# Attention with q and k laid out transposed on the host, and products of 48 instead of 64 columns

## The chip, the cores and the metric

The program runs on one core of a Trainium2 chip. The metric is the device time of one execution in microseconds (us). The engines are named as in the profile: PE (TensorE, with its weight loads as PEld), DVE (VectorE), ACT (ScalarE), POOL (GpSimd) and SP (SyncE, which here issues most of the DMAs). Every engine works through its own instructions in the order in which the program was written.

## The reference

Three parts follow each other. The first is a delta-rule attention over 4 batches, 8 heads, 768 steps and 48 dimensions; the second and third are a routed mixture of experts (8 experts, 2 per token) and a dense layer of 2048 hidden units.

```python
k_n = k / (np.linalg.norm(k, axis=-1, keepdims=True) + 1e-06)
for t in range(S):
    kt, vt, bt = (k_n[:, :, t], v[:, :, t], beta[:, :, t, None])
    y[:, :, t] = np.einsum('bhd,bhde->bhe', q[:, :, t], state)
    v_old = np.einsum('bhde,bhd->bhe', state, kt)
    state = state + bt[:, :, :, None] * np.einsum('bhd,bhe->bhde', kt, vt - v_old)
...
x = np.ascontiguousarray(attn_out.transpose(0, 2, 1, 3)).reshape(B * S, H * D)
x = _moe_ref(x=x, **moe_kwargs)
return _moe2_ref(x=x, **moe2_kwargs)
```

## The kernel before

The attention is computed in blocks of 64 steps. There are 12 such blocks in a sequence, and two batches share a block's work (one in partitions 0 to 63, one in 64 to 127), so 24 blocks n = 0 to 23 are done, and even and odd n are two independent recurrences. Per block the program does the following, each step a function in emit_attention.

- load_kq (L166) brings q and k of the block in as tiles kq, with the step in the partition. trans (L191) turns four heads at a time on PE (L197) and copies them out of PSUM into mq (two copies, L201, on ACT). So mq holds q and k with the head dimension in the partition. A block takes two calls of trans.
- gram (L203), two calls per block, multiplies k by q and k (L214). ACT copies the q part into mq (two copies, L219) and the k part into gd and goff (L222, L223). DVE then adds the second half into gd (L224); this last step is put off until the next flush. The PSUM tiles gm have two buffers.
- inverse_ops (L242) inverts the 32 x 32 triangular blocks of four n on DVE (head L256, the products L296 and L304, the tail L321 and L322). Its some 130 instructions are spread between the other work by run(t), which hands out credit according to the table PE_US, times PACE; what is left is put out at the end of each group of four blocks. merge1 and merge2 combine two 32-blocks (PE L347 and L368, DVE L370).
- The recurrence is ks (L389), solve (L399) and update (L410), and output (L422) gives y; each is 16 matrix products, 32 PE instructions, and ACT copies their results out of PSUM. In ks, solve and output 64 columns move, of which 48 are used; in update 48 move.
- v_norm (L377) and the mask (L237) run on POOL; the router's transposes, logits and the DVE steps of the routing (L820 on) are mixed in. warm (L434) puts unneeded matrix products on PE; the tables F, FG and FL say how many and where.

At the start the first four blocks are loaded, turned and multiplied, POOL fills the constant halves of mq (init_m, L120) and clears T (L255), and the inverse of the first four blocks runs while grams of blocks 4 to 7 are done (20.6 to 59 us). Then the loop over n in steps of two does the recurrence for n and n + 1 and the gram of n + 8 and n + 9. From 310 us on come the last four blocks and the handover to the experts, and from 385 us on the experts and the dense layer, in which PE is nearly always busy.

Of the kernel before, what the change touches and what calls it, by code (L numbers as in the profile page):

```python
# [16 lines left out]
DP = 64  # L17
# [9 lines left out]
TA = 2  # L27
# [11 lines left out]
PE_US = dict(ks=1.26, solve=1.26, update=1.0, output=1.26, trans=0.43, gram=0.94, merge1=0.6, merge2=0.6)  # L39
# [52 lines left out]
def emit_attention(ctx, tc, q, k, v, beta, const, rt, moe):  # L92
# [11 lines left out]
    NK, NQ, NM, NU = 4, 4, 10, 4  # L104
    tok = [slice(0, 64), slice(64, 128)]
    st = [slice(64, 128), slice(0, 64)]
    kbd = [pk.tile([128, NH, 2, HD], F32, name=f"kbd{i}") for i in range(NK)]
    kq = [pr.tile([128, NH, 2, DP], F32, name=f"kq{i}") for i in range(NQ)]
    mq = [[(pr if i >= 4 else pk).tile([128, NH, 2, CH], F32, name=f"mq{b}{i}") for i in range(NM)] for b in range(2)]
    us = [[pk.tile([128, NH * HD + 16], F32, name=f"us{b}{i}") for i in range(NU)] for b in range(2)]  # L110
    rz = [[pk.tile([128, NH * HD + 16], F32, name=f"rz{b}{i}") for i in range(2)] for b in range(2)]

    def init_k(i):
        for b in range(2):
            nc.vector.tensor_copy(out=kbd[i][st[b], :, b, :],
                                  in_=eye[st[b], 0:HD].unsqueeze(1).to_broadcast([64, NH, HD]))

    def init_m(i):
        for b in range(2):
            nc.gpsimd.affine_select(out=mq[b][i][tok[b], :, 1, :],  # L120
# [4 lines left out]
    for i in range(NQ):  # L125
        (nc.vector if i < 2 else nc.gpsimd).memset(kq[i][:, :, :, HD:DP], 0.0)
# [10 lines left out]
    def cols(t, h):  # L137
        return t[:, h * HD:h * HD + 64]
# [379 lines left out]
    for n in range(4):  # L518
        load_kq(n)
# [1105 lines left out]
```

## Time and profile before

| | us |
|---|---|
| median of 3 runs | 1234.82 |
| lowest and highest run | 1229.9 and 1238.5 |
| span of the profiled execution | 1245.6 |
| busy in it: PE, DVE, ACT, POOL | 1163.7, 711.4, 548.2, 311.6 |

The page gives no other time for the profiled execution than its span; it lies outside the three timed runs, 10.8 us above their median. Busy times are averages over parts with different limits, so they have to be read by stretch. In a wait row the left side is the engine and line that stood still, the right side what it was waiting for last.

### The profile page before, as it was taken

How to read it: one execution, taken by the hardware profiler on the slowest of the kernel's cores; microseconds unless marked ns; L12 is line 12 of the kernel's file. 1: busy time of each engine (PE TensorE's matmuls, PEld its weight loads, DVE VectorE, ACT ScalarE, POOL GpSimd, SP SyncE). 2: the span in 40 equal slices, each digit the busy share in tenths (PEclk: the TensorE clock that was granted, in tenths of full speed). 3: DMA queues.
4: the chain of work that ended last, by engine and by line, in shares of the span. 5: the costliest groups of instructions: out<-in, count | busy, mean ns of one | idle time of the engine just before them, and what ended most of it. 6: DMA issues, size and time to landing. Idle time of an engine off the chain costs nothing. (4 is left out here: it accounts for less than half of the span.)

```text
span 1245.6 us, 26717 instructions
## 1 busy us (share of the span) xinstructions
PE 1163.7 (93%) x10743; PEld 1051.9 (84%) x10760; DVE 711.4 (57%) x1923; ACT 548.2 (44%) x1133; POOL 311.6 (25%) x399
## 2 busy tenths in 40 slices
PE   7798888787878999999999999989999999999998
PEld 4476767665757999999999999978989898998988
DVE  7988789879363777675757453436242433425150
ACT  5776777763453433232324233337242433434150
POOL 7242244555244513232231313015000000000000
PEclk9998899988889999999999999999999999999999
DMA  4634334322325545444534321262202010110000
GB/s 85 103 79 92 66 73 92 73 40 42 91 77 190 159 161 173 164 144 155 188 136 160 116 90 56 67 200 78 70 7 64 13 60 17 45 33 2 24 1 26
DMA packets 146530, 109.47 MB, mean 88 GB/s; under 512 B 110104, under 2 KB 131941, under 8 KB 145638
## 3 DMA queue, kind: packets, MB, share of 16 engines
q1 hardware_dynamic: 137446, 86.39, 25.1%
q0 software_dynamic: 8448, 19.70, 4.9%
q8 instruction: 85, 1.39, 0.5%
q10 hardware_dynamic: 512, 1.67, 0.4%
q14 instruction: 39, 0.32, 0.1%
HBM read 82.43 MB, written 26.08 MB: 87 GB/s over the span
## 5 line engine op out<-in xcount | busy, mean ns | idle before, releaser
L1197 PE MATMUL yp<-w2h,ht 128*128 128x384 f32 x832 | 221.2, 340 | 0.0
L1197 PE MATMUL yp<-w2l,ht 128*128 128x384 f32 x448 | 150.2, 335 | 0.0
L1197 PEld LDWEIGHTS yp<-w2h,ht 128*128 128x128 f32 x832 | 148.5, 188 | 0.3
L987 POOL DMA_INDIRECT y<-ys,idp x56 | 65.0, 1161 | 301.8 <-DVE ys L1206 223.5
L1174 PE MATMUL hp<-xth,w1h 128*128 128x416 f32 (+2 forms) x384 | 136.9, 357 | 0.6 <-ACT xth L1115 0.6
L1174 PE MATMUL hp<-xtl,w1h 128*128 128x416 f32 (+2 forms) x384 | 136.2, 355 | 0.0
L1174 PE MATMUL hp<-xth,w1l 128*128 128x416 f32 (+2 forms) x384 | 135.8, 354 | 0.0
L1535 PE MATMUL yp<-woh,gh 128*128 128x384 f32 x384 | 130.4, 340 | 0.0
L1535 PE MATMUL yp<-woh,gl 128*128 128x384 f32 x384 | 129.1, 336 | 0.0
L1535 PE MATMUL yp<-wol,gh 128*128 128x384 f32 x384 | 129.1, 336 | 0.0
L1177 ACT ACTIVATE ht<-hp 128x416 fp32r<-128x416 f32 (+2 forms) x128 | 66.4, 519 | 133.1 <-PE hp L1174 118.4
L1180 DVE SCALAR_TENSOR_TENSOR ht<-hp,ht 128x352 fp32r<-128x352 f32 (+3 forms) x192 | 79.3, 441 | 63.5 <-ACT ht L1177 61.3
L1503 PE MATMUL hp<-xh,wih 128*128 128x512 f32 x288 | 112.8, 392 | 2.7 <-DVE three L1489 2.7
L304 DVE TENSOR_TENSOR T<-T,tmp 128x1 f32<-128x1 f32 (+9 forms) x540 | 113.8, 258 | 0.4
L1503 PE MATMUL hp<-xl,wih 128*128 128x512 f32 x288 | 112.9, 392 | 0.0
L1503 PE MATMUL hp<-xh,wil 128*128 128x512 f32 x288 | 112.7, 391 | 0.0
L1512 DVE TENSOR_TENSOR gl<-r,gh 128x512 fp32r<-128x512 f32 x96 | 66.5, 693 | 78.4 <-ACT gh L1511 78.4
L1506 ACT ACTIVATE r<-hp,three 128x512 f32<-128x512 f32 x96 | 66.2, 690 | 89.0 <-PE hp L1503 89.0
L1508 DVE SCALAR_TENSOR_TENSOR r<-r,hp 128x512 f32<-128x512 f32 x96 | 65.4, 681 | 53.9 <-ACT r L1506 53.9
L1197 PEld LDWEIGHTS yp<-w2l,ht 128*128 128x128 f32 x448 | 84.1, 188 | 0.0
L214 PE MATMUL gm<-mq 64*64 64x128 f32 (+1 forms) x896 | 60.8, 266 | 19.6 <-ACT mq L201 11.0
L1542 ACT ACTIVATE os<-yp 128x384 f32<-128x384 f32 x23 | 11.3, 492 | 153.4 <-PE yp L1535 153.4
(221 smaller groups left out, 2300.5 us busy)
## 6 DMA issues: line engine op xcount, KB each, us to landing
r<-in_moe_w_dram SPq DMA_DIRECT2D x16, 768.0 KB
r<-in_moe_w_dram SPq DMA_DIRECT2D x21, 512.0 KB
yg<-y SPq DMA_DIRECT2D x24, 384.0 KB
wd_r<-in_moe_w_in_dram SPq DMA_DIRECT2D x6, 1024.0 KB
wd_r<-in_moe_w_out_dram SPq DMA_DIRECT2D x8, 768.0 KB
kq<-in_q_dram SPq DMA_DIRECT2D x48, 96.0 KB
kq<-in_k_dram SPq DMA_DIRECT2D x48, 96.0 KB
v<-in_v_dram SPq DMA_DIRECT2D x48, 96.0 KB
```

Of the source, the lines that this page charges most:

```text
L214: nc.tensor.matmul(gm[tok[b], h, lo:hi], lhsT=m[:, 1, :], rhs=m[:, lo // 64:hi // 64, :], start=True, stop=True)
L304: nc.vector.tensor_tensor(out=T[:, lo:hi, 0:w], in0=T[:, lo:hi, 0:w], in1=tmp[jj % 2][:, (lo - w) * w:(hi - w) * w].rearrange("p (t k) -> ...
L987: return nc.gpsimd.indirect_dma_start(out=y, out_offset=bass.IndirectOffsetOnAxis(ap=idx, axis=0), in_=src, in_offset=None, bounds_check=y ...
L1174: nc.tensor.matmul(p[:, 0:w], lhsT=a[:, k, fs], rhs=b[:, k, c], start=(i == 0), stop=(i == 3 * KD - 1))
L1177: nc.scalar.activation(out=h[:, c], in_=p[:, 0:w], func=ACTF.Relu)
L1180: nc.vector.scalar_tensor_tensor(out=h[:, rest(lo, hi)], in0=p[:, lo - c.start:hi - c.start], scalar=0.0, in1=h[:, lo:hi].bitcast(F32), op ...
L1197: nc.tensor.matmul(p[0:2 * m if pair else m, 0:DM], lhsT=a, rhs=b[:, f, :], start=f == i == 0, stop=f == FT - 1 and i == len(terms) - 1)
L1503: nc.tensor.matmul(p, lhsT=a[:, k, fs], rhs=b[:, k, :], start=(i == 0), stop=(i == 3 * KD - 1))
L1506: nc.scalar.activation(out=r, in_=p, func=ACTF.Relu, bias=three)
L1508: nc.vector.scalar_tensor_tensor(out=r, in0=r, scalar=6.0, in1=p, op0=ALU.min, op1=ALU.mult)
L1512: nc.vector.tensor_tensor(out=gl[:, f, :], in0=r, in1=gh[:, f, :].bitcast(F32), op=ALU.subtract)
L1535: nc.tensor.matmul(p[:, 0:DM], lhsT=a[:, f, c], rhs=b[:, f, :], start=(i == 0), stop=(i == 3 * FT2 - 1))
```

## The change

The host now lays the inputs out. q and k arrive as one array with the head dimension in the rows (48 rows, padded with zeros to 64 for the first 12 blocks), and load_qk writes them straight into mq. The function trans and its copies go, and so do the tiles kq and what cleared them. mq is kept for 12 blocks instead of 10, and init_m runs for each of them; q and k now lie in two separate halves of the tile. ks, solve and output move 48 columns instead of 64. k, v, beta, the noise and the router's weights come in the order in which the tiles hold them, with fewer loads. The entry for trans leaves the table PE_US; PACE, F, FG, FL and the counts of warm are as they were.

```diff
-TA = 2
...
-PE_US = dict(ks=1.26, solve=1.26, update=1.0, output=1.26, trans=0.43, gram=0.94, merge1=0.6, merge2=0.6)
+PE_US = dict(ks=1.26, solve=1.26, update=1.0, output=1.26, gram=0.94, merge1=0.6, merge2=0.6)
...
-    NK, NQ, NM, NU = 4, 4, 10, 4
+    NK, NM, NU = 4, 12, 4
     tok = [slice(0, 64), slice(64, 128)]
     st = [slice(64, 128), slice(0, 64)]
-    kbd = [pk.tile([128, NH, 2, HD], F32, name=f"kbd{i}") for i in range(NK)]
-    kq = [pr.tile([128, NH, 2, DP], F32, name=f"kq{i}") for i in range(NQ)]
-    mq = [[(pr if i >= 4 else pk).tile([128, NH, 2, CH], F32, name=f"mq{b}{i}") for i in range(NM)] for b in range(2)]
-    us = [[pk.tile([128, NH * HD + 16], F32, name=f"us{b}{i}") for i in range(NU)] for b in range(2)]
-    rz = [[pk.tile([128, NH * HD + 16], F32, name=f"rz{b}{i}") for i in range(2)] for b in range(2)]
+    kbd = [pk.tile([128, 2, NH, HD], F32, name=f"kbd{i}") for i in range(NK)]
+    mq = [[(pk if i in [n % NM for n in range(NT - 4, NT)] else pr).tile([128, 2, NH, CH], F32, name=f"mq{b}{i}") for i in range(NM)] for b in range(2)]
+    us = [[pk.tile([128, NH * HD], F32, name=f"us{b}{i}") for i in range(NU)] for b in range(2)]
+    rz = [[pk.tile([128, NH * HD], F32, name=f"rz{b}{i}") for i in range(2)] for b in range(2)]
...
-    for i in range(NQ):
-        (nc.vector if i < 2 else nc.gpsimd).memset(kq[i][:, :, :, HD:DP], 0.0)
...
-        return t[:, h * HD:h * HD + 64]
+        return t[:, h * HD:(h + 1) * HD]
...
-    def bp_c(n):
-        return n % 2, n // 2
-
     def load_k(n):
-        bp, c = bp_c(n)
         for b in range(2):
-            nc.sync.dma_start(out=kbd[n % NK][tok[b], :, b, :],
-                              in_=k[2 * bp + b, :, c * CH:(c + 1) * CH, :].rearrange("h t d -> t h d"))
-
-    def load_kq(n):
-        bp, c = bp_c(n)
-        for i, src in enumerate((q, k)):
-            for b in range(2):
-                nc.sync.dma_start(out=kq[n % NQ][64 * i:64 * i + 64, :, 1 - b, 0:HD],
-                                  in_=src[2 * bp + b, :, c * CH:(c + 1) * CH, :].rearrange("h t d -> t h d"))
+            nc.sync.dma_start(out=kbd[n % NK][tok[b], b], in_=k[n, b])
+
+    def load_qk(n, part=slice(0, 2)):
+        rows = 64 if n < NM else HD
+        for b in range(2):
+            nc.sync.dma_start(out=mq[b][n % NM][st[b].start:st[b].start + rows, part], in_=qk[n, b, 0:rows, part])
 
     def load_v(n):
-        bp, c = bp_c(n)
         t = wk.tile([128, NH, HD], F32, tag="v", name="v", bufs=4)
-        for b in range(2):
-            nc.sync.dma_start(
-                out=t[tok[b]], in_=v[2 * bp + b, :, c * CH:(c + 1) * CH, :].rearrange("h t d -> t h d"))
+        nc.sync.dma_start(out=t, in_=v[n])
         vt[n] = t
 
     def load_beta(g):
         t = wk.tile([128, 32], F32, tag="beta", name="beta")
-        for cc in range(2):
-            for b in range(2):
-                for blk in range(2):
-                    s0 = (2 * g + cc) * CH + blk * 32
-                    p0 = b * 64 + blk * 32 + cc * 16
-                    nc.sync.dma_start(
-                        out=t[p0:p0 + 16, :],
-                        in_=beta[:, :, s0:s0 + 32].rearrange("(bp b) h t -> b bp h t", b=2)[b])
+        nc.sync.dma_start(out=t, in_=beta[g])
         beta_t[g] = t
-
-    def trans(n, hh):
-        first = n < 4
-        tp = ps2.tile([128, 4, 2, CH], F32, tag="ch" if first and hh else "tp", name="tp")
-        for h in range(4):
-            nc.tensor.transpose(tp[:, h].rearrange("p k t -> p (k t)"),
-                                kq[n % NQ][:, 4 * hh + h].rearrange("p k d -> p (k d)"), ident)
-        for b in range(2):
-            copy = nc.vector.tensor_copy if first and hh else nc.scalar.copy
-            copy(out=mq[b][n % NM][st[b], 4 * hh:4 * hh + 4], in_=tp[st[b]])
 
...
-                m = mq[b][n % NM][st[b], 4 * hh + h]
+                m = mq[b][n % NM][st[b], :, 4 * hh + h]
...
-                nc.scalar.copy(out=mq[b][n % NM][tok[b], hs, 0, :], in_=gm[tok[b], :, 0:64])
+                nc.scalar.copy(out=mq[b][n % NM][tok[b], 0, hs, :], in_=gm[tok[b], :, 0:64])
...
-                nc.tensor.matmul(p[tok[b], h, :], lhsT=mq[b][n % NM][:, h, 1, :], rhs=cols(us[b][n % NU], h),
+                nc.tensor.matmul(p[tok[b], h, 0:HD], lhsT=mq[b][n % NM][:, 1, h, :], rhs=cols(us[b][n % NU], h),
...
-                nc.tensor.matmul(p[tok[b], h, :], lhsT=x[:, h, :], rhs=cols(rz[b][n % 2], h), start=True, stop=True)
+                nc.tensor.matmul(p[tok[b], h, 0:HD], lhsT=x[:, h, :], rhs=cols(rz[b][n % 2], h), start=True, stop=True)
...
-                nc.tensor.matmul(p[o:o + HD, h, 0:HD], lhsT=kbd[n % NK][:, h, b, :], rhs=cols(us[b][n % NU], h)[:, 0:HD],
+                nc.tensor.matmul(p[o:o + HD, h, 0:HD], lhsT=kbd[n % NK][:, b, h, :], rhs=cols(us[b][n % NU], h),
...
-                nc.tensor.matmul(p[tok[b], h, :], lhsT=mq[b][n % NM][:, h, 0, :], rhs=cols(us[b][n % NU], h),
+                nc.tensor.matmul(p[tok[b], h, 0:HD], lhsT=mq[b][n % NM][:, 0, h, :], rhs=cols(us[b][n % NU], h),
...
     for n in range(4):
-        load_kq(n)
+        load_qk(n, slice(1, 2))
     load_beta(0)
-    for i in range(2, NM + 2):
-        init_m(i % NM)
+    for n in range(4):
+        load_qk(n, slice(0, 1))
+    for i in range(NM):
+        init_m(i)
     warm(P0)
-    for i in range(TA):
-        trans(*divmod(i, 2))
     for i in range(8):
-        if TA > 1:
-            flush()
-        if i + TA < 8:
-            trans(*divmod(i + TA, 2))
         flush()
         gram(*divmod(i, 2), "g")
         warm(P1[i])
     flush()
     load_beta(1)
     for n in range(4):
-        load_kq(n + 4)
+        load_qk(n + 4)
     for m in range(4):
         load_v(m)
         if m < 2:
             gram(n, hh, "m")
             warm(P2)
             run(PQ)
-    trans(4, 0)
     for i in range(8, 16):
         n, hh = divmod(i, 2)
-        if i < 15:
-            trans(*divmod(i + 1, 2))
         warm(P3)
         gram(n, hh)
         run(PP)
         flush()
         if hh and n < 6:
-            load_kq(n + 4)
+            load_qk(n + 4)
             v_norm(n - 4)
         if i == 8:
             load_beta(2)
         if a % 4 == 2 and a // 4 + 1 < NG:
             load_beta(a // 4 + 1)
         for i in range(2):
-            live(load_kq, a + 2 + i)
+            live(load_qk, a + 2 + i)
...
-        live(trans, a, 0)
...
-        live(trans, a, 1)
...
-        live(trans, a + 1, 0)
...
-        live(trans, a + 1, 1)
...
+def laid_out(x):
+
+    import numpy as np
+
+    def tiles(t):
+        t = np.asarray(t).reshape(2, 2, NH, SEQ // CH, CH, HD)
+        return t.transpose(3, 0, 1, 2, 4, 5).reshape(NT, 2, NH, CH, HD)
+
+    q, k, v = (tiles(x[n]) for n in "qkv")
+    qk = np.zeros((NT, 2, 64, 2, NH, CH), np.float32)
+    for i, t in enumerate((q, k)):
+        qk[:, :, 0:HD, i] = t.transpose(0, 1, 4, 2, 3)
+    beta = np.asarray(x["beta"]).reshape(2, 2, NH, NG, 2, 2, 32).transpose(3, 1, 5, 4, 0, 2, 6)
+    noise = np.asarray(x["moe_noise"]).reshape(2, 2, SEQ // CH, CH, EXP).transpose(1, 3, 2, 0, 4)
+    wgn = np.concatenate([x["moe_w_gate"], x["moe_w_noise"]], 1).reshape(KD, 128, 2 * EXP).transpose(1, 0, 2)
+    out = dict(
+        qk=qk, k=k.transpose(0, 1, 3, 2, 4), v=v.transpose(0, 1, 3, 2, 4).reshape(NT, 128, NH, HD),
+        beta=beta.reshape(NG, 128, 32), wgn=wgn, noise=noise.reshape(128, NT, EXP))
+    out.update((n, x[n]) for n in ("moe_w1", "moe_w2", "moe2_w_in", "moe2_w_out"))
+    return out
```

The first place is ACT in the loop, from the results of solve to those of update: in iteration n = 8 before, and in the same iteration now (us, tp, gm and sd are the tiles of solve's result, the turned q and k, the gram and update's result).

```order
L153 COPY us_153<-u 64x384 [waits PE_49,Pool_49]
L153 COPY us_157<-u 64x384 [waits Pool_49]
L153 COPY us_154<-u 64x384 [waits PE_49,Pool_49]
L153 COPY us_158<-u 64x384 [waits Pool_49]
L201 COPY mq_139<-tp 64x512 [waits PE_49]
L201 COPY mq_149<-tp 64x512
L219 COPY mq_139<-gm 64x4x64 [waits PE_49]
L219 COPY mq_149<-gm 64x4x64
L222 ACTIVATE gd<-gm,half 128x128
L223 COPY goff<-gm 128x128
L153 COPY us_155<-sd 48x384 [waits PE_49]
L153 COPY us_159<-sd 48x384
```

```order
L148 COPY us_153<-u 64x384 [waits PE_49,Pool_49]
L148 COPY us_157<-u 64x384 [waits Pool_49]
L148 COPY us_154<-u 64x384 [waits PE_49,Pool_49]
L148 COPY us_158<-u 64x384 [waits Pool_49]
L187 COPY mq_133<-gm 64x256 [waits PE_49]
L187 COPY mq_145<-gm 64x256
L190 ACTIVATE gd<-gm,half 128x128
L191 COPY goff<-gm 128x128
L148 COPY us_155<-sd 48x384 [waits PE_49]
L148 COPY us_159<-sd 48x384
L148 COPY us_156<-sd 48x384 [waits PE_49]
L148 COPY us_160<-sd 48x384
```

Before, two copies of turned tiles stand between solve's results and the gram's four rows; now the gram's rows follow at once, and update's results two rows sooner.

The second place is POOL at the start, from the first clearing to the memset of T, before and now.

```order
L126 MEMSET kq_131 128x16x16 [waits Pool_49]
L126 MEMSET kq_132 128x16x16
L133 MEMSET us_153 128x400
...
L120 AFFINE_SELECT mq_133<-zero 64x8x64
L120 AFFINE_SELECT mq_143<-zero 64x8x64
L120 AFFINE_SELECT mq_134<-zero 64x8x64
L120 AFFINE_SELECT mq_144<-zero 64x8x64
L255 MEMSET T 128x1024 [waits Pool_49]
```

```order
L86 MEMSET half 32x1 x3
L128 MEMSET us_153 128x384 [waits Pool_49]
...
L117 AFFINE_SELECT mq_138<-zero 64x512
L117 AFFINE_SELECT mq_150<-zero 64x512
L117 AFFINE_SELECT mq_139<-zero 64x512
L117 AFFINE_SELECT mq_151<-zero 64x512
L117 AFFINE_SELECT mq_140<-zero 64x512
L117 AFFINE_SELECT mq_152<-zero 64x512
L223 MEMSET T 128x1024 [waits Pool_49]
```

The two memsets of kq are gone ahead of the first row of us, and four more fills of mq stand ahead of the memset of T (24 instead of 20).

## Rows read from the trace of the kernel before

**Rows 1.** Busy time by stretch (start:end, length, busy us of each engine, clock, DMA, GB/s).

```profile
0.00:20.61 20.61, 15.76 (x190) 10.28 (x192) 12.30 (x27) 10.19 (x26) 18.71 (x46) 1.00 0.43 79
20.61:59.15 38.54, 29.67 (x347) 18.21 (x348) 36.07 (x145) 28.54 (x72) 11.89 (x22) 0.99 0.57 98
59.15:310.13 250.98, 208.79 (x4599) 168.75 (x4610) 212.68 (x901) 170.65 (x416) 110.57 (x166) 0.89 0.37 71
160.71:185.38 24.67, 20.70 (x481) 17.12 (x480) 20.36 (x74) 19.90 (x47) 11.29 (x17) 0.93 0.46 82
185.38:211.95 26.57, 22.66 (x548) 18.64 (x547) 24.32 (x114) 19.96 (x51) 14.13 (x23) 1.00 0.43 78
98.08:108.32 10.24, 6.28 (x87) 5.49 (x85) 9.49 (x30) 4.77 (x14) 4.00 (x6) 0.56 0.19 46
310.13:385.00 74.87, 61.16 (x1027) 50.44 (x1023) 40.13 (x140) 37.26 (x73) 28.44 (x43) 0.89 0.23 70
385.00:1245.50 860.50, 848.27 (x4594) 804.25 (x4592) 410.19 (x713) 301.60 (x549) 141.97 (x124) 1.00 0.29 94
```

**Rows 2.** Waits of DVE in the loop, 59.15 to 310.13 (total us, times, longest).

```profile
DVE gd L224 <- ACT goff L223: 14.9, 11, 2.4
DVE x L370 <- PE mg L368: 8.2, 3, 4.6
DVE x L370 <- ACT rt_ls L836: 3.1, 2, 1.9
DVE rt_pos L907 <- PE rk L904: 2.9, 2, 1.9
DVE x L370 <- ACT mq L201: 2.3, 1, 2.3
```

**Rows 3.** Groups by line in the same stretch (busy us, mean ns).

```profile
L201 ACT COPY mq<-tp 64x512 f32<-64x512 f32 x64 | 37.1, 580 | 2.2 <-PE wp L434 0.6 <-PE tp L197 0.6
L197 PE MATMUL tp<-ident,kq 128*128 128x128 f32 x128 | 20.9, 286 | 1.5 <-ACT mq L201 1.5
```

**Rows 4.** Waits of PE in the same stretch.

```profile
PE gm L214 <- ACT mq L201: 10.9, 19, 1.7
PE sd L410 <- ACT us L153: 1.9, 4, 0.6
```

**Rows 5.** Timeline of one gram in the loop (start us, us).

```profile
174.50 1.18 ACT L201 COPY mq<-tp 64x512 f32<-64x512 f32 x2
175.59 0.74 ACT L219 COPY mq<-gm 64x256 f32<-64x256 f32 x2
176.34 0.37 ACT L222 ACTIVATE gd<-gm,half 128x128 f32<-128x128 f32 x1
176.61 0.26 ACT L223 COPY goff<-gm 128x128 f32<-128x128 f32 x1
176.90 0.35 DVE L224 SCALAR_TENSOR_TENSOR gd<-gm,half,gd 128x128 f32<-128x128 f32 x1 [1.76 <-ACT goff L223]
```

**Rows 6.** Timeline: two calls of solve, two of update, one of output at half clock.

```profile
88.60 2.21 PE L399 MATMUL u<-rz,x 128*64 128x64 f32 x64
92.34 1.65 PE L410 MATMUL sd<-us,kbd 128*48 128x48 f32 x64
103.37 1.98 PE L422 MATMUL y<-us,mq 128*64 128x64 f32 x32
```

**Rows 7.** Timeline of the start: POOL, and DVE's copy that follows.

```profile
3.84 0.99 POOL L126 MEMSET kq<- 128x256 f32 x2
9.96 14.06 POOL L120 TENSOR_SCALAR_AFFINE_SELECT mq<-zero 64x512 f32<-64x512 f32 x20
24.08 0.95 POOL L255 MEMSET T<- 128x1024 f32 x1
26.03 0.20 DVE L288 COPY T<-sm 128x32 f32<-128x32 f32 x1
```

**Rows 8.** Waits of DVE from 20.61 to 59.15.

```profile
DVE gd L224 <- ACT goff L223: 1.4, 2, 0.8
```

More of the change, by code (lines that the diff above doesn't have):

```diff
@@ L16 @@
 HD = 48
-DP = 64
 NH = 8
@@ L89, in emit_attention_consts, with emit_attention @@
     return half, eye, zero, wz
-def emit_attention(ctx, tc, q, k, v, beta, const, rt, moe):
+def emit_attention(ctx, tc, qk, k, v, beta, const, rt, moe):
     nc = tc.nc
@@ L102, in emit_attention @@
     m0, m1 = half[:, 0:1], half[:, 1:2]
[L104 removed]
+    NK, NM, NU = 4, 12, 4
     tok = [slice(0, 64), slice(64, 128)]
     st = [slice(64, 128), slice(0, 64)]
[L107 to L111 removed]
+    kbd = [pk.tile([128, 2, NH, HD], F32, name=f"kbd{i}") for i in range(NK)]
+    mq = [[(pk if i in [n % NM for n in range(NT - 4, NT)] else pr).tile([128, 2, NH, CH], F32, name=f"mq{b}{i}") for i in range(NM)] for b in range(2)]
+    us = [[pk.tile([128, NH * HD], F32, name=f"us{b}{i}") for i in range(NU)] for b in range(2)]
+    rz = [[pk.tile([128, NH * HD], F32, name=f"rz{b}{i}") for i in range(2)] for b in range(2)]
     def init_k(i):
         for b in range(2):
[L115 removed]
+            nc.vector.tensor_copy(out=kbd[i][st[b], b],
                                   in_=eye[st[b], 0:HD].unsqueeze(1).to_broadcast([64, NH, HD]))
@@ L119, in init_m @@
         for b in range(2):
-            nc.gpsimd.affine_select(out=mq[b][i][tok[b], :, 1, :],
+            nc.gpsimd.affine_select(out=mq[b][i][tok[b], 1],
                                     in_=zero[tok[b]].unsqueeze(1).to_broadcast([64, NH, CH]),
@@ L235, in mask @@
         for b in range(2):
-            m = mq[b][n % NM][tok[b], :, 0, :]
+            m = mq[b][n % NM][tok[b], 0]
             nc.gpsimd.affine_select(out=m, in_=m, pattern=[[0, NH], [1, CH]], compare_op=ALU.is_gt,
@@ L511, in live @@
                     NT - 16 <= tok < NT - 12 and fn in beat and cur >= NT - 8 or \
-                    NT - 12 <= tok < NT - 8 and cur >= NT - 6 and fn not in (load_v, load_k, v_norm):
+                    NT - 12 <= tok < NT - 8 and cur >= NT - 6 and fn not in (load_v, load_k, load_qk, v_norm):
                 rt.moves.pop(0)[1]()
@@ L745, with __init__ @@
 class Router:
-    def __init__(self, ctx, tc, noise, w_gate, w_noise, const, xd, ids):
+    def __init__(self, ctx, tc, noise, wgn, const, xd, ids):
         self.tc, self.nc, self.const, self.xd, self.ids = tc, tc.nc, const, xd, ids
-        self.src = noise, w_gate, w_noise
+        self.src = noise, wgn
         kp = ctx.enter_context(tc.tile_pool(name="rt_k", bufs=1))
@@ L773, in setup @@
         self.ps = ps
-        noise, w_gate, w_noise = self.src
-        nc.sync.dma_start(out=self.wgn[:, :, 0:EXP], in_=w_gate.rearrange("(k p) e -> p k e", p=128))
-        nc.sync.dma_start(out=self.wgn[:, :, EXP:2 * EXP], in_=w_noise.rearrange("(k p) e -> p k e", p=128))
-        for b in range(2):
-            for bp in range(2):
-                nc.sync.dma_start(
-                    out=self.nz[64 * b:64 * b + 64].rearrange("p (c k) e -> p c k e", k=2)[:, :, bp, :],
-                    in_=noise[(2 * bp + b) * SEQ:(2 * bp + b + 1) * SEQ].rearrange("(c p) e -> p c e", p=CH))
+        noise, wgn = self.src
+        nc.sync.dma_start(out=self.wgn, in_=wgn)
+        nc.sync.dma_start(out=self.nz, in_=noise)
         nc.gpsimd.memset(self.ones, 1.0)
@@ L1572, with kernel @@
 @with_exitstack
-def kernel(ctx, tc, q, k, v, beta, w_gate, w_noise, noise, w1, w2, w_in, w_out, out):
+def kernel(ctx, tc, qk, k, v, beta, wgn, noise, w1, w2, w_in, w_out, out):
     nc = tc.nc
@@ L1583 @@
         const = emit_consts(nc, cp)
-        rt = Router(ctx, tc, noise, w_gate, w_noise, const, xd, ids)
+        rt = Router(ctx, tc, noise, wgn, const, xd, ids)
         m1 = Moe1(tc, rt, w1, w2, y, const)
         with ExitStack() as c2:
-            x_last = emit_attention(c2, tc, q, k, v, beta, const, rt, m1)
+            x_last = emit_attention(c2, tc, qk, k, v, beta, const, rt, m1)
         with ExitStack() as c2:
@@ L1595 @@
             m2.emit(c2)
-_INS = ['q', 'k', 'v', 'beta', 'moe_w_gate', 'moe_w_noise', 'moe_noise', 'moe_w1', 'moe_w2', 'moe2_w_in', 'moe2_w_out']
+def laid_out(x):
[15 more added lines that the diff above has]
+    return out
 _OUTS = [((3072, 384), 'float32')]
@@ L1610 @@
     arrays, args = {}, []
-    for name in _INS:
-        a = _np.ascontiguousarray(inputs[name])
+    for name, a in laid_out(inputs).items():
+        a = _np.ascontiguousarray(a)
         if a.dtype == _np.float64:
```

## The prediction

> **What bounds the kernel now.** I read the busy times by stretch first [rows 1]. From 385 us to the end PE is busy for 848.3 of 860.5 us at clock 1.00, with work that the change does not touch. So the change is worth what it takes off the first 385 us, in four stretches: the start (20.6 us), the first inverse (38.5), the loop (251.0) and the last four blocks (74.9).
>
> In the loop no engine fills the time: DVE is busy for 212.7 of 251.0 us, PE for 208.8 at a mean granted clock of 0.89, ACT for 170.7. Two neighbouring passes show how it alternates [rows 1]: from 185.38 to 211.95 DVE works 24.3 of 26.6 us and is the bound; from 160.71 to 185.38 it works 20.4 of 24.7 and stands for the other 4.3. The waits of DVE say for whom [rows 2]: 14.9 us for ACT's copy goff, 2.3 for ACT's copy of a turned tile, 3.1 for ACT's rt_ls, together 20.3 us with ACT as the last to come; 8.2 us are for PE's merge and 2.9 for the rank product. The timeline of one gram shows what lies in front of goff [rows 5]: 1.18 us of turned copies, then 0.74, 0.37 and 0.26 us, and DVE starts after 1.76 us of waiting. PE for its part waited 10.9 us, 19 times, for those copies before a gram [rows 4]. So the loop's time is DVE's work of 212.7 us plus 38.3 us in which DVE has nothing to do, mostly since the chain trans, copy, gram, copy comes late.
>
> **The change, part by part.** I add differences to the median of the runs. The profiled span of 1245.6 us lies 10.8 above it and 7.1 above the highest run, so the rows are about 1% long; on a difference of some 18 us that is 0.2 us, which I leave out.
>
> Loop. The transposes on PE go, 128 instructions with 20.9 us of busy time, and 64 copies with 37.1 us on ACT [rows 3]. The narrower products: solve takes 2.21 us for two calls with 64 columns, update 1.65 for two with 48 [rows 6], so a call saves 0.28 us at full clock if the moving columns set the pace, and nothing if something else does, since update's weights are narrower as well. I take 0.28, since the two calls differ in little else. Ten passes with two calls of each of the three functions, less ks of blocks 0 and 1 (no product) and the last two outputs (after 310 us), are 56 calls, so 15.7 us; PE loses 36.6 of 208.8 us in all. The Trainium skill ("TensorE: Matmul & The Clock Gate", Back-to-back issue gap) lists one and the same step, about 25 ns, for anything from 1 to 64 columns; by it the narrower products would save nothing, and my sum would be 1219. The trace speaks against it: 2.21 us over 64 instructions is 35 ns, 1.65 is 26 [rows 6].
>
> None of these 36.6 us counts by itself, because DVE is the longer engine: what counts is how much of DVE's 38.3 idle us goes. In front of a gram's goff PE loses a transposing step and ACT 1.18 us of copies, some 1.7 us together, against waits for goff that average 14.9 / 11 = 1.4 us. Where DVE waits for the turned copy itself (2.3 us) the wait goes altogether; for rt_ls (3.1 us) ACT's queue is shorter. Not all of it can be kept. Behind solve a transpose of four heads was the cover while ACT copied solve's result: update already waited 1.9 us, up to 0.6 each [rows 4], and without the cover this grows by about the length of the transposes, 20.9 / 32 = 0.65 us in each of nine passes, 6 us on PE, though PE has that to spare now. PE will also reach the end of a group earlier and stand until the inverse is done. I take three quarters of the 20.3 us, 15 us. Bounds: 0, if every wait is only renamed, and 31.4, if all five rows of waits go.
>
> The order of DVE's work hardly changes: leaving trans out of the table hands out 4 x 0.43 x 0.95 = 1.6 us less credit in a pass, so each gram's last step on DVE stands one to three steps of the inverse earlier than before; this suits a PE that is earlier, and I cost it at nothing. If PE were not earlier, DVE would wait for these steps, some 1.6 us in a pass.
>
> Start. The first gram no longer waits for transposes, but that is covered. DVE's copy into T at 26.03 needs POOL's memset of T, which ended at 25.03 [rows 7], 1.0 us before. Twenty fills of mq took 14.06 us, 0.70 each; four more add 2.8, the memsets of kq that go take off 0.99: net 1.8, so the memset ends at 26.9 and DVE loses 0.8 us. Between 0 (if the contiguous fills run faster) and 1.8 (if DVE's side slips as well). Eight copies that DVE did itself here go too, and buy nothing.
>
> First inverse. DVE is busy for 36.1 of 38.5 us [rows 1]; the 1.4 us of waiting for goff [rows 8] go with the transposes and copies of these blocks: 1.4 us, between 0 and the 2.5 us that DVE stands in all.
>
> Last four blocks. Fourteen calls with 0.28 us less each (32 instructions a call; 4 of ks, 4 of solve and 6 of output) are 4 us on PE; DVE and ACT are only half busy here and the calls alternate with copies, so I take half, 2 us, between 0 and 4.
>
> Loads. PE's waits on q and k exist only at the start, where the first warm products cover them; the new loads are fewer and in longer pieces. In the loop a load of q and k now waits for the output of two blocks before, as the last reader of its tile, and has a whole pass until its gram. The loads of v and k stand behind it in SP's queue, and they too are wanted a pass later. Cost zero; if that cover were gone, PE's gram and POOL's v_norm would wait.
>
> Sum: -15 + 0.8 - 1.4 - 2 = -17.6 us, so 1234.8 - 17.6 = **1217 us**.
>
> **The rivals.**
>
> All waits go (chance 0.13). If DVE ran through, the loop would fall by 31.4, the last blocks by 4, the first inverse by 1.4: 1234.8 - 31.4 - 4 - 1.4 + 0.8 = 1199 us. For it: PE and ACT lose twice as much as DVE waits. Against: 8.2 us of the waits are for the merge, which the change does not shorten, and it begins only when the inverse has ended.
>
> The waits are handed on (0.23). DVE's work is 212.7 us whatever PE does. In the pass that DVE fills, only 2.3 us are free at most [rows 1]; there PE gains nothing and stands instead. If the same holds in the other passes, because PE's new idle time and update's lost cover put the merge later, a quarter of the 20.3 us stays: 5 + 1.4 - 0.8 = 5.6 us, and 1229.
>
> The clock turns it round (0.08, slower). PE's clock is 0.89 in the loop: that is half speed (1.2 instead of 2.4 GHz) for 22% of 251 us, 54 us. Such a stretch follows a standstill: after PE had waited 3 us for DVE at the end of a group, 98.08 to 108.32 shows 0.56, and one call of output took 1.98 us [rows 1, 6], against 1.1 for a call of solve at full speed. So of every us at half speed 0.44 us are extra. With 36.6 us less to do PE stands more often. It comes back to its old length when 36.6 / 0.44 = 83 us more run at half speed, at a mean clock of 0.73; from there on each further us costs 0.44 us. At 0.65 over the loop, another 39 us, the loop is 17 us longer than now: 1234.8 + 17 = 1252, or 1249 with the small terms of the other stages. Against it: the pass from 185.38 held 1.00, although PE stood 3.9 us of 26.6 [rows 1], and part of the time that PE now saves comes back as shorter passes.
>
> The change does what it says: the instruction streams show that the transposes and copies are gone, so that they don't go is no case.
>
> **How the numbers follow.** The forecast has 0.56, with a range of its own of 1208 to 1224. 1217 is its middle. The range of 1203 to 1232 takes in most of the renamed case, the better half of the case in which all waits go, and the bounds of the start and the last blocks; outside lie the case of the clock and the far end of the gain. About 1% (12 us) is what a measurement of this kernel can tell from no change, since its three runs span 8.6 us. Faster by over 1% means below 1222.5: 0.13 and most of 0.56, together 0.66. Within 1%: the renamed case and the rest of the forecast, 0.26. Slower: 0.08.
>
> **What would show it.** In the new profile the loop's waits of DVE for goff should be down from 14.9 to some 4 us, those of PE for turned copies gone, DVE's busy time the same 213 us in a loop of about 236, the same two calls of solve near 1.65 us, and the memset of T ending near 26.9. Update's waits for ACT should have grown. The prediction is wrong if DVE's waits only change their partner, if the granted clock of the loop falls towards 0.73, or if the part after 385 us changes its length.

## The result, and the profile after

The changed kernel takes 1241.0 us (median of 17 runs, 1238.4 to 1251.4) against 1234.3 for the kernel before (17 runs on the same chip, 1229.8 to 1239.2). The ratio is 1.0067 with an interval of 1.0048 to 1.0085: it became slower by 0.7%, where 17.6 us less had been forecast.

The busy times by stretch of the kernel after (start:end, length, busy us of PE, PEld, DVE, ACT and POOL with their instructions, granted clock, DMA share, GB/s) answer to [rows 1]:

```profile
0.00:15.82 15.82, 11.18 (x157) 6.95 (x160) 6.78 (x17) 5.65 (x18) 14.22 (x38) 1.00 0.62 173
15.82:60.31 44.49, 27.86 (x315) 16.90 (x317) 38.31 (x145) 19.60 (x56) 18.90 (x32) 0.85 0.59 132
60.31:310.33 250.02, 198.87 (x4435) 169.80 (x4450) 218.70 (x901) 135.89 (x350) 111.75 (x166) 0.80 0.28 64
82.00:94.00 12.00, 10.94 (x201) 9.75 (x203) 10.14 (x43) 4.53 (x13) 3.14 (x4) 0.57 0.49 96
310.33:385.00 74.67, 63.83 (x1080) 54.75 (x1079) 40.44 (x141) 37.63 (x74) 29.48 (x44) 0.90 0.25 78
385.00:1238.60 853.60, 843.61 (x4569) 800.09 (x4567) 409.80 (x712) 301.51 (x549) 140.76 (x123) 1.00 0.28 94
```

The profiled execution of before was a long one (1245.6 us, its loop 250.98). A second profile of the same kernel (the first experiment below) lies at 1233.2 us, close to the median, and is the one to compare loops with. Its loop:

```profile
61.24:306.51 245.27, 207.97 (x4577) 167.59 (x4578) 211.22 (x901) 170.17 (x414) 111.09 (x166) 0.89 0.39 72
```

So the work did go: ACT is busy for 34 us less in the loop, and no transposes are left on PE. But the loop is 4.8 us longer. Two numbers stand out. PE's granted clock is 0.80 where it was 0.89, and DVE is busy for 218.7 us, 7.5 more, although the loop's DVE program is the same 901 instructions.

The waits of DVE in the loop of the kernel after (us in total, times, longest), against [rows 2]:

```profile
DVE x L338 <- PE mg L336: 12.9, 8, 4.4
DVE gd L192 <- ACT goff L191: 12.2, 8, 2.1
DVE rt_t L820 <- ACT rt_t L814: 1.3, 1, 1.3
DVE rt_pos L859 <- PE rk L856: 0.2, 1, 0.2
```

and those of PE, against [rows 4]:

```profile
PE mg L315 <- DVE x L338: 20.4, 9, 5.9
PE gm L182 <- DVE gd L192: 13.8, 6, 4.1
PE y L390 <- ACT x L148: 7.9, 8, 1.6
```

The waits for turned copies are gone on both engines. DVE still waits for goff and, longer than before, for the merge; PE, which used to wait for ACT's copies, now stands for DVE.

Two calls of solve, then two of update, in PE's timeline of the kernel after (start us, us):

```profile
278.22 1.14 PE L367 MATMUL u<-rz,x 128*64 128x48 f32 x32
279.61 1.14 PE L367 MATMUL u<-rz,x 128*64 128x48 f32 x32
280.90 1.92 PE L378 MATMUL sd<-us,kbd 128*48 128x48 f32 x64 [0.15 <-ACT us L148]
```

A call of solve with 48 moving columns takes 1.14 us; two calls with 64 took 2.21 us [rows 6], and a single one with 64 takes 1.15 us in the second experiment below. The narrower products are not shorter.

### The profile page after: what moved, and what is told of

It reads as the page before. It is cut to its first block, busy times and chain, and to the rows that moved or that the text cites. A ratio compares the mean times of both kernels' runs of the same rounds, so it can differ in the third digit from the quotient of the medians.

```text
span 1238.7 us, 26043 instructions
## 1 busy us (share of the span) xinstructions
PE 1145.3 (92%) x10547; PEld 1048.5 (85%) x10568; DVE 714.0 (58%) x1913; ACT 500.3 (40%) x1045; POOL 315.1 (25%) x401
## 2 busy tenths in 40 slices
DMA packets 54688, 111.02 MB, mean 90 GB/s; under 512 B 9048, under 2 KB 36901, under 8 KB 53798
## 5 line engine op out<-in xcount | busy, mean ns | idle before, releaser
L272 DVE TENSOR_TENSOR T<-T,tmp 128x1 f32<-128x1 f32 (+9 forms) x540 | 116.6, 264 | 0.4
L182 PEld LDWEIGHTS gm<-mq 64*64 64x64 f32 x896 | 51.0, 152 | 41.0 <-DVE gd L192 32.3
```

The costliest lines, as they stand in the source:

```text
L182: nc.tensor.matmul(gm[tok[b], h, lo:hi], lhsT=m[:, 1, :], rhs=m[:, lo // 64:hi // 64, :], start=True, stop=True)
L272: nc.vector.tensor_tensor(out=T[:, lo:hi, 0:w], in0=T[:, lo:hi, 0:w], in1=tmp[jj % 2][:, (lo - w) * w:(hi - w) * w].rearrange("p (t k) -> ...
```

## The experiments

All ratios are to the kernel before, run on the same chip as the kernel in question; one chip was slower for every kernel that ran there (update at 64 columns, ACT's edit on before, and the two that add to it; before took 1247.5 us), so times are compared through the ratio.

**Before again.** 

> The kernel before, unchanged, timed against itself, for the spread of the profile. All theories: ratio 1.000 within 0.002. Its profile tells how far one execution's stages scatter: first expert product at 346 to 356 us (353.8 in the profile before), granted clock of the loop 0.85 to 0.92.

1233.7 us, ratio 0.9990 (0.9974 to 1.0007). Its loop row stands above; the clock, 0.89, lies in the expected range. The experts' first product comes at 344.2 us, outside the expected 346 to 356 and 9.6 us ahead of the first profile's 353.8: so far apart can two executions of one kernel be at that place.

**64 columns again in the changed kernel.**

```diff
-        return t[:, h * HD:(h + 1) * HD]
+        return t[:, h * HD:h * HD + 64]
...
-                nc.tensor.matmul(p[tok[b], h, 0:HD], lhsT=x[:, h, :], rhs=cols(rz[b][n % 2], h), start=True, stop=True)
+                nc.tensor.matmul(p[tok[b], h, :], lhsT=x[:, h, :], rhs=cols(rz[b][n % 2], h), start=True, stop=True)
```

The second pair of lines is solve's; ks and output are changed alike, us and rz are 16 columns wider, and update is held at 48.

> The changed kernel with 64 moving columns again in ks, solve and output. Clock theory (narrow products cost PE the same time, 1.14 against 1.15 us a call, and only make its clock fall): faster than the changed kernel by 2 to 6 us, ratio to before 1.001 to 1.004, clock of the loop above 0.80. Rival (narrow products do save time, and the loss lies elsewhere): slower than the changed kernel, ratio 1.008 or more. If columns matter to neither: ratio 1.0067.

1232.6 us, ratio 0.9994 (0.9980 to 1.0007), faster than the changed kernel by more than the 2 to 6 us expected. The loop of this kernel:

```profile
59.44:302.94 243.50, 194.11 (x4468) 162.00 (x4470) 218.58 (x901) 135.55 (x350) 112.08 (x166) 0.85 0.29 66
```

The whole loss comes from the narrower columns: the order of the program is the same in both, and the intervals of 0.9994 and 1.0067 are apart. With 64 columns the rest of the change is worth nothing that can be measured. The clock stands at 0.85, between before (0.89) and after (0.80). That order does not hang on three profiled executions: every timed run has its clock over the whole execution on record, and it lies at 0.969 to 0.979 in before, 0.954 to 0.965 with 64 columns and 0.930 to 0.945 with 48, without overlap. One call of solve in this kernel (start us, us), against 1.14 us with 48 columns, and the longest waits of its DVE:

```profile
274.47 1.15 PE L367 MATMUL u<-rz,x 128*64 128x64 f32 x32
```

```profile
DVE x L338 <- PE mg L336: 9.8, 7, 4.8
DVE gd L192 <- ACT goff L191: 8.0, 7, 1.9
```

**48 columns alone, in the kernel before.**

```diff
-        return t[:, h * HD:h * HD + 64]
+        return t[:, h * HD:(h + 1) * HD]
...
-                nc.tensor.matmul(p[tok[b], h, :], lhsT=x[:, h, :], rhs=cols(rz[b][n % 2], h), start=True, stop=True)
+                nc.tensor.matmul(p[tok[b], h, 0:HD], lhsT=x[:, h, :], rhs=cols(rz[b][n % 2], h), start=True, stop=True)
```

Again solve's lines stand for those of ks and output too.

> The kernel before, with 48 instead of 64 moving columns in ks, solve and output, and nothing else of the change (q and k are still turned on PE, all tiles as they were). Theory (the columns lower the granted clock and buy no time): a call of solve stays at 1.1 to 1.15 us at full speed, the loop's clock falls from 0.89 to about 0.84, and the time is 4 to 9 us above before (ratio 1.003 to 1.007). Rival (the columns cost only in company with the rest of the change, where PE has less to do): ratio 0.999 to 1.001. Rival of the prediction (each call 0.28 us shorter): 8 us faster, ratio 0.994.

1250.8 us, ratio 1.0123 (1.0093 to 1.0153). The loss is there without any other part of the change, and larger than expected. Its loop:

```profile
60.64:316.98 256.34, 218.08 (x4569) 177.96 (x4578) 212.13 (x902) 171.39 (x414) 110.67 (x166) 0.84 0.37 69
```

DVE's and ACT's work is that of before; PE is busy for 10 us more at the lower clock, with fewer columns to move. The clock over the whole execution is 0.948 to 0.962 in its five runs, against 0.966 to 0.978 in the runs of before beside them.

**48 columns in one product at a time** (the changed kernel, 64 in the other two).

> The changed kernel with 64 columns in solve and output, and 48 in ks alone. The kernel with 64 in all three stands at a ratio of 0.9994 to before, the one with 48 in all three at 1.0067. Theory (each of the three costs alike, about a third of 0.0073): ratio 1.001 to 1.003, loop clock 0.83 to 0.84. Rival (one product carries it): 0.999 to 1.000 if it is not ks, 1.005 or more if it is.

> 48 columns in solve alone, 64 in ks and output. Theory (each a third): ratio 1.001 to 1.003. Rival (one product carries it, solve, as PE stands for ACT's copy of its result right behind it): 1.005 or more here, 0.999 to 1.000 in the other two.

> 48 columns in output alone, 64 in ks and solve. Theory (each a third): ratio 1.001 to 1.003. Rival (one product carries it, output, as PE's longest waits for DVE, in front of the merge of the next group, come right behind it): 1.005 or more here, 0.999 to 1.000 in the other two.

ks 1.0014 (0.9994 to 1.0034), solve 1.0033 (1.0013 to 1.0054), output 1.0027 (1.0006 to 1.0048). Over 0.9994 these are 0.0020, 0.0039 and 0.0033, together 0.0092 against 0.0073 for all three at once. No single product carries the loss, as none reaches 1.005. Only solve's interval lies clear of that of the kernel with 64 columns (0.9980 to 1.0007); output's touches it and that of ks overlaps it, so equal shares fit but are not shown. The clock over the whole execution falls in all three: its median is 0.951, 0.950 and 0.953, against 0.959 with 64 columns and 0.940 with 48 in all.

**64 columns in update too, in the kernel before.**

```diff
-nc.tensor.matmul(p[o:o + HD, h, 0:HD], ..., rhs=cols(us[b][n % NU], h)[:, 0:HD], ...)
+nc.tensor.matmul(p[o:o + HD, h, :], ..., rhs=cols(us[b][n % NU], h), ...)
```

> The kernel before, with 64 instead of 48 moving columns in update too (16 columns of the next head that nobody reads), nothing else. Theory (more columns at the same step hold the granted clock up): two calls of update still take 1.65 us at full speed, the loop's clock rises from 0.89 to 0.91 or more, and the time falls by 2 to 6 us, ratio 0.995 to 0.998. Rival (update's step follows its columns, 1.65 us become 2.2): slower by 2 to 5 us. Rival (48 columns are bad only in the three products): ratio 0.999 to 1.001.

Ratio 0.9998 (0.9976 to 1.0020), loop clock 0.90: nothing. The premise of the first theory, an unchanged step, doesn't hold here. The two calls of update in the second profile of before, and then in this kernel (x64 instructions: shortest, middle and longest in ns, first and last start in us):

```profile
L410 PE MATMUL sd<-us,kbd x64: 208/208/243, 94.5 to 95.9; 128*48 128x48 f32 x64
```

```profile
L410 PE MATMUL sd<-us,kbd x64: 218/219/257, 94.5 to 96.3; 128*48 128x64 f32 x64
```

From the first to the last start 1.4 us become 1.8, over 63 steps 22 ns become 29. Update's weights are 48 wide, and there the moving columns do lengthen the step. One call of solve, whose weights are 64 wide, read in the same way with 64 columns (changed kernel) and with 48 (the kernel after):

```profile
L367 PE MATMUL u<-rz,x x32: 222/222/270, 274.5 to 275.4; 128*64 128x64 f32 x32
L367 PE MATMUL u<-rz,x x32: 222/222/257, 279.6 to 280.5; 128*64 128x48 f32 x32
```

0.9 us over 31 steps is 29 ns, whether 64 or 48 columns move. In these four rows the step goes with the wider of the two, weights or moving columns. So this run cannot say what free columns would do to the clock.

**Idle transposes in place of the ones that went** (four at each of the four places in a pass, in the changed kernel).

```diff
+    def fill():
+        tp = ps2.tile([128, 4, 128], F32, tag="tp", name="tp")
+        for h in range(4):
+            nc.tensor.transpose(tp[:, h], ident, ident)
```

> The changed kernel with four idle transposes of a constant on PE at each of the four places of the loop where trans stood; no copies, no credit for them. Clock theory, if such work holds the clock: loop clock back near 0.89 and ratio to before 0.998 to 1.002. If transposes cost PE time without holding the clock: ratio 1.010 or more. Order theory (the missing credit for trans puts steps of DVE too early): as the changed kernel or slower, 1.007 to 1.012.

1247.7 us, ratio 1.0106 (1.0081 to 1.0132), loop 258.87 us at clock 0.82. They gave back 0.02 of clock and cost more than that: PE's busy time rose from 198.9 to 221.4 us. The theory of the order (the missing credit for trans) had named the same range, so this run does not set it aside; no run put that credit back.

**An earlier start** (POOL's 24 fills of mq moved behind the first clearing of T).

```diff
-    for i in range(NM):
-        init_m(i)
     warm(P0)
...
     run(4.0)
+    for i in range(NM):
+        init_m(i)
     rt.setup(wk, ps2)
```

> The changed kernel with the 24 fills of mq put behind the first memset of T on POOL. Start theory (DVE's 4.5 us wait for that memset is on the path): the inverse begins about 4.5 us sooner and the kernel is 4 us faster than the changed one, ratio to before 1.003. Rival (given back later in the loop, or POOL's fills slow DVE's steps): no more than 1 us faster, ratio 1.006 to 1.007.

1241.7 us, ratio 1.0062 (1.0045 to 1.0079), as without it. The loop began at 57.78 instead of 60.31 us and then took 253.73 us at clock 0.76: in this execution the 2.5 us were lost again, as the loop ended at 311.51 instead of 310.33. It was the longest of the six runs (1246.6 us), so the 0.76 may be lower than usual; that the gain does not reach the end stands on the ratio.

**Without POOL's mask** for blocks 8 to 23 (changed kernel, 64 columns).

```diff
-            else:
+            elif n < 8:
                 mask(n)
```

> The changed kernel with 64 columns, and POOL's mask left out for blocks 8 to 23 (so y is not the reference's). Theory (DVE's 7 us more of work in the loop come from POOL's masks, which now run while DVE works and no longer while it waits for goff): DVE's busy time in the loop falls from 218.6 to 206 to 209 us, the products' mean from 379 to 340 to 355 ns, and the time falls by 6 to 12 us against the kernel with 64 columns (1232.6), ratio to before 0.989 to 0.994. Rival (the longer DVE operations come from the new layout of the tiles or from v_norm): DVE stays at 216 us or more and the ratio at 0.998 to 1.000.

1229.7 us, ratio 0.9946 (0.9925 to 0.9968). Its loop:

```profile
59.90:298.11 238.21, 186.68 (x4477) 159.13 (x4492) 208.64 (x901) 136.00 (x351) 90.67 (x134) 0.86 0.31 68
```

DVE's two costliest groups in the loop, busy us and mean ns, with the mask and then without it:

```profile
L272 DVE TENSOR_TENSOR T<-T,tmp 128x72 f32<-128x72 f32 (+35 forms) x450 | 97.5, 264 | 0.3
L264 DVE TENSOR_TENSOR tmp<-A,T 128x31 f32<-128x31 f32 (+15 forms) x155 | 58.8, 379 | 0.3
```

```profile
L272 DVE TENSOR_TENSOR T<-T,tmp 128x72 f32<-128x72 f32 (+35 forms) x450 | 88.9, 245 | 0.3
L264 DVE TENSOR_TENSOR tmp<-A,T 128x31 f32<-128x31 f32 (+15 forms) x155 | 56.6, 365 | 0.3
```

DVE's busy time fell from 218.58 to 208.64 us, all of it in these two groups (10.8 us together). So POOL's masks lengthen DVE's instructions. The gain in time is at the low edge: 0.9946 just misses the 0.989 to 0.994 of the theory, the products' mean of 365 ns misses 340 to 355, and the loop fell by only 5.3 us, as DVE waited more. How, one piece of the timeline of the kernel with 64 columns shows (start us, us):

```profile
98.12 0.38 DVE L264 TENSOR_TENSOR tmp<-A,T 128x220 f32<-128x220 f32 x1
...
99.31 1.74 POOL L345 TENSOR_TENSOR us<-v,rows 64x384 f32<-64x384 f32 x2
99.34 0.34 DVE L192 SCALAR_TENSOR_TENSOR gd<-gm,half,gd 128x128 f32<-128x128 f32 x1
99.60 0.76 DVE L264 TENSOR_TENSOR tmp<-A,T 128x207 f32<-128x207 f32 x1
...
101.39 0.35 DVE L264 TENSOR_TENSOR tmp<-A,T 128x192 f32<-128x192 f32 x1
```

The product of 207 elements, which stands between one of 220 with 0.38 us and one of 192 with 0.35, takes 0.76 us while POOL's v_norm runs. I held every DVE instruction of the loop against the lower quartile of its shape and added up what lies above: about 32 us in before, about 40 with the change and 64 columns, and all but some 2 us of each lie beside a POOL instruction. Most of it lies beside v_norm in both kernels; beside the mask it is about 7 and 12 to 13 us, and that is where the growth is. The traces of the two kernels also show why: the masks last 29.5 us in the second profile of before and 30.2 us with 64 columns, but DVE was busy during 18.8 us of them before and during 24.7 us now. Of the 10.7 us in which DVE stood while a mask ran, 5.6 were in front of a gram's second half (the wait for goff) before; now it is 0.7 of 5.5. Both the mask and goff follow ACT's copies of mq [rows 5].

**ACT's freed time spent on DVE's work** (changed kernel, 64 columns).

```diff
+            else:                       # gram, blocks 8 to 23
+                nc.scalar.copy(out=d, in_=gm[:, :, 64:96])
+                nc.scalar.copy(out=goff[n][:, hs, :], in_=gm[:, :, 64:96])
+                for p in (slice(32, 64), slice(96, 128)):
+                    nc.scalar.copy(out=d[p], in_=gm[p, :, 96:128])
...
+            nc.scalar.copy(out=x[:, :, 32:64], in_=X[:, 8 * j:8 * j + 8, :])        # merge1
...
+        if not last4[0]:                # merge2, in place of DVE's step
+            for b in range(2):
+                p = slice(64 * b, 64 * b + 32)
+                nc.scalar.mul(out=x[p, :, 32:64], in_=mg[p], mul=-1.0)
+            return
```

> The changed kernel with 64 columns, and ACT's freed time spent on two pieces of DVE's work: for blocks 8 to 23 the second half of gd, and in the loop the second half of x, are put together by ACT with copies by partition, so that DVE neither does these steps (10.6 + 9.5 us in the loop) nor waits in front of them (8.0 for goff, 9.8 for the merge). Theory (the loop is DVE's work plus what DVE waits for): the loop falls from 243.5 to 215 to 228 us, ACT's busy time there rises from 136 to 175 to 190 us, the time is 1205 to 1220, ratio 0.976 to 0.989. Rival (PE and its clock set the loop by now, and a shorter loop only lowers the clock further): loop 236 us or more, ratio 0.994 to 1.000.

1220.6 us, ratio 0.9896 (0.9859 to 0.9933): faster than both kernels, though just short of the 0.976 to 0.989 expected. Its loop:

```profile
60.33:287.93 227.60, 180.19 (x4543) 153.60 (x4559) 203.43 (x849) 173.15 (x481) 113.09 (x166) 0.91 0.31 71
```

The loop is 15.9 us shorter than with 64 columns alone, at the upper end of what was expected; the profiled execution is the fastest of the six. DVE's waits in front of a gram's second half and of the merge are gone with the steps, but DVE stands 24.2 us all the same, against 24.9, now for the rank products (8.6) and gd (6.0) above all. The gain is that of DVE's work, which fell by 15.2 us.

**The same edit on the kernel before.**

> The kernel before, with the two pieces of DVE's work given to ACT as in e6_wide_act, and nothing of the change. It tells whether the gain of e6_wide_act needs the ACT time that the change frees. Theory that it does (ACT would then carry 208 of some 240 us in the loop, and PE is as long as before): ratio 0.995 to 1.003. Rival (the gain is that of the edit alone): ratio 0.987 to 0.993, as with the change.

Ratio 1.0151 (1.0125 to 1.0177): worse than expected by either. Its waits of DVE in the loop:

```profile
DVE rt_pos L919 <- PE rk L916: 42.7, 3, 16.4
DVE A L262 <- ACT gd L231: 11.7, 2, 7.8
```

ACT is busy for 204.1 us there, PE waits 16.2 us for the turned copies (9.9 before), and DVE reaches the end of its steps and stands. So the edit pays only together with the change: the two together gain 1.0%, either one alone nothing or less. That it is the freed time of ACT and PE which the edit needs fits these rows; no run separates it from the rest of the change.

**The same edit with 48 columns.**

> The changed kernel itself (48 columns) with the same two pieces of DVE's work given to ACT. Theory (the narrow columns cost by the clock whatever DVE does): 4 to 9 us slower than the same edit with 64 columns, at a loop clock that is lower by 0.03 to 0.06. Rival (the narrow columns only cost while PE stands still for DVE): the two within 2 us of each other.

1248.6 us, ratio 1.0088 (1.0052 to 1.0124), by the ratios 24 us slower than with 64 columns, where 4 to 9 had been expected. Its loop, and one stretch of 8 us of it; then the stretch with 64 columns that begins at the same call of output:

```profile
59.25:322.94 263.69, 226.29 (x4435) 194.96 (x4452) 195.70 (x849) 172.55 (x474) 110.64 (x166) 0.68 0.28 61
131.00:139.00 8.00, 8.00 (x159) 7.36 (x161) 8.00 (x51) 3.65 (x9) 0.00 (x0) 0.50 0.62 150
```

```profile
124.20:130.00 5.80, 5.80 (x180) 5.22 (x182) 5.80 (x34) 4.28 (x11) 0.00 (x0) 1.00 0.54 150
```

PE is busy throughout both, with 159 instructions in 8.0 us at clock 0.50 and 180 in 5.8 us at 1.00. PE's timeline at the start of the two stretches, with 48 and then with 64 columns:

```profile
127.71 1.14 PE L402 MATMUL y<-us,mq 128*64 128x48 f32 x32
130.97 1.95 PE L402 MATMUL y<-us,mq 128*64 128x48 f32 x32 [2.12 <-ACT x L148]
```

```profile
120.88 1.15 PE L402 MATMUL y<-us,mq 128*64 128x64 f32 x32
124.20 1.15 PE L402 MATMUL y<-us,mq 128*64 128x64 f32 x32 [2.17 <-ACT x L148]
```

With 48 columns the second call takes 1.95 instead of 1.14 us after PE has stood 2.12 us for ACT; with 64 columns PE stands 2.17 us before the same call, and it takes 1.15 us as the first one did. So the same standstill cost the clock here in one kernel and not in the other. The profiles are one of the longer executions (1255.2 us) and the fastest (1217.2), so the loops' 36 us overstate the usual difference; but the clock over the whole execution is 0.912 to 0.933 in the nine runs with 48 columns and 0.957 to 0.971 in the six with 64.

**64 columns in update in addition, and the earlier start.**

> The kernel of e6_wide_act (changed kernel, 64 columns, two pieces of DVE's work on ACT) with 64 columns in update as well. Theory (columns hold the clock): the loop's clock rises from 0.91 to 0.93 to 0.97, the loop falls from 227.6 to 219 to 225, the time is 1213 to 1218, ratio 0.981 to 0.987. Rival (the waits, and not the clock, set this loop now): within 2 us of e6_wide_act.

> The kernel of e10 with POOL's 24 fills of mq behind the first clearing of T, as in e3_early_t, which took 2.5 us off the start there and lost them in the loop. Theory (with the clock held up, the earlier start reaches the end): 2 to 3 us faster than e10. Rival (the loop gives it back through a lower clock, as in e3_early_t): the same as e10 or slower.

> The kernel of e6_wide_act with POOL's 24 fills of mq behind the first clearing of T, 48 columns in update as before. Theory (the earlier start reaches the end where the clock holds, as from e10 to e11, 0.9922 to 0.9896): ratio 0.984 to 0.988. Rival (the loop gives the 2.5 us back): 0.988 to 0.992, as e6.

Update at 64: 0.9922 (0.9901 to 0.9943), no better than 0.9896 without and short of the 0.981 to 0.987 expected; its step grows, and its clock over the whole execution (0.958 to 0.969) is no higher than without (0.957 to 0.971). With the earlier start on top: 0.9896 (0.9870 to 0.9923). The earlier start without update's columns: 1219.4 us, ratio 0.9876 (0.9839 to 0.9913), against 0.9896; the intervals overlap in both pairs, so whether the start's 2 us reach the end is not settled.

## Why the prediction was wrong, step by step

By the ratios the result lies 26 us above the forecast (1.0067 against 1217 / 1234.8). Some 11 of these belong to the narrower products (9 us lost where a gain of 2 had been forecast), some 15 to the loop's waits and DVE's work: with 64 columns, where the rest of the change stands alone, the ratio is 0.9994 where 0.987 had been forecast.

**The narrower products, 0.28 us a call: the step that failed and turned the sign.** It compared solve with update and put the difference down to the moving columns. The two also differ in the width of their weights, 64 and 48; the prediction named that, and still took the full difference. Measured: no gain a call (1.14 us against 1.15). The 15.7 us of PE time in the loop and the 4 in the last four blocks were never there. The 35 and 26 ns of the prediction divide the busy time, with the last instruction's run in it, by the number of instructions; from start to start it is 29 ns in solve and 22 in update. The rule that I set aside, from the Trainium skill ("TensorE: Matmul & The Clock Gate", Back-to-back issue gap), one step of about 25 ns for 1 to 64 columns, gives the outcome for solve, though at 29 ns; for update the rows differ from it (22 and 29 ns for 48 and 64 columns).

**The clock: the rival that came true, by a way that I had not seen.** I let it fall because PE has less to do, and gave it 0.08. It fell twice. Removing transposes and copies took it from 0.89 to 0.85, half speed for 22% of 245.3 us (54 us) becoming 30% of 243.5 (73). Taking off columns that cost no time took it to 0.80, 40% of 250.0 (100 us). At the prediction's 0.44 us for each us at half speed this is an estimate of 8 us for the first step and 12 for the second; the loop grew by 6.5 in the second and PE's busy time by 4.8, so that price is too high there. Three pairs show the second step with the program's order unchanged: 0.89 to 0.84 (before), 0.85 to 0.80 (changed), 0.91 to 0.68 (with ACT's edit), at 11.1, 6.5 and 36.1 us more loop. Each loop is one profiled execution; but the ratios of the three pairs have intervals that do not overlap, and neither do the clocks of their runs over the whole execution. What it is about the columns that the chip answers to, these runs do not tell.

**The loop's waits, three quarters of 20.3 us: the step that failed by the most.** The mechanism was half right. With 64 columns DVE stands 24.9 us (243.50 less 218.58) instead of 34.1 (245.27 less 211.22), so 9 of the expected 15 us went. Goff fell to 8.0 us in that kernel, not to 4, and to 12.2 at 48 columns, where more of PE's work runs at the lower clock. The quarter that I left for waits that are handed on was too little: PE stands 20 us before a merge and 14 before a gram, for DVE. So with 64 columns the rival in which the waits are handed on came nearest, 1229 against 1232.6. How much of what DVE still waits comes from the missing credit for trans, which I costed at nothing, no run tested.

**DVE's work of 212.7 us, taken as fixed.** With 64 columns it rose by 7.4 us, which took back most of those 9. The prediction counted DVE's instructions, not what runs beside them: some 5 of the 7.4 us lie beside POOL's masks.

**Update's cover.** Its waits for ACT did not grow: 1.9 us before [rows 4], 0.2 after; I put this down to ACT's shorter queue, which no run tested. So the 6 us of PE time that the prediction named there did not come.

**Start and first inverse.** POOL's clearing of T ended at 27.1 us (forecast 26.9), DVE's copy behind it began at 27.12 instead of 26.03. That is 1.1 us where 0.8 had been forecast. The loop began at 60.31 us, between the 59.15 and 61.24 of the two profiles of before, so the sum of the start's terms is not to be told from their scatter. The rows:

```profile
13.49 12.59 POOL L117 TENSOR_SCALAR_AFFINE_SELECT mq<-zero 64x512 f32<-64x512 f32 x18
26.14 0.95 POOL L223 MEMSET T<- 128x1024 f32 x1
```

```profile
27.12 0.20 DVE L256 COPY T<-sm 128x32 f32<-128x32 f32 x1 [4.52 <-POOL T L223]
```

The 1.4 us at the first inverse did not come: goff is still waited for 1.0 us there, and the clock is 0.85 instead of 0.99, in a stretch in which PE stood 11.7 us before one gram, for DVE. DVE's work grew from 36.1 to 38.3 us.

**Last four blocks, 2 us.** From the end of the loop to the experts' first product it is 43.7 and 37.7 us in the two profiles of before, 39.8 after and 40.3 with 64 columns: no gain that shows, where 2 us are less than the two executions of before differ.

**Loads, zero.** Right: 54,688 packets instead of 146,530, and in the loop no wait of PE or DVE that names them.

## What to carry to other kernels

Before a narrower operand is costed as a gain, compare two rows that differ in nothing else; where the weights are the wider of the two, dropped columns bought no time, and here the three products together lost 0.7% by it, at a lower clock. When work is removed from an engine that is not the bound, ask which engine inherits the wait and hand the freed time to the bound: here the removal alone, with 64 columns kept, was worth nothing, and the same removal with two of DVE's steps moved to ACT 1.0%, or 1.2% with the earlier start. Check the granted clock of the stretch after every removal on PE.

## What the runs showed of the hardware

Moving 48 instead of 64 columns in products whose step stays at 29 ns lowered the granted clock of the loop in three pairs of kernels, in one from 0.91 to 0.68 with the order unchanged. I had thought of the clock as following PE's standstills alone; but a standstill of 2.1 to 2.2 us before the same call was followed by 0.50 with 48 columns and by 1.00 with 64.

DVE's instructions grow while POOL works: one product took 0.76 us between neighbours of 0.38 and 0.35, and some 32 to 40 us of the loop's DVE time are such excess. The Trainium skill ("SBUF — State Buffer", Who interferes with whom) says that a DVE instruction with two inputs in SBUF contends with a POOL instruction that reads SBUF, over ports that one of them locks. The trace agrees in kind: the product has two such inputs, and beside the same POOL row a DVE instruction with one of its two inputs in PSUM (L192, 0.34 us, the median of its 32 in the loop) kept its length. How long one of them holds the other up, these rows do not tell.
